# Two VectorE operations as one instruction, and the gate's products moved behind the sequence stage, in a gated FNet and Mish kernel

## The chip, the cores and the metric

The kernel runs on one core of a Trainium2 chip. The metric is the device time of one execution in microseconds. A program of this kind has five engines that work side by side, each through its own list of instructions in order: TensorE (PE in the profile; its weight loads are PEld), VectorE (DVE), ScalarE (ACT), GpSimd (POOL, here used to issue stores) and SyncE (SP, here used to issue loads). A matmul writes to one of eight banks of PSUM; VectorE and ScalarE read and write both PSUM and SBUF.

## The reference

With x of 2048 tokens by 640 features, four transform matrices, a dense layer of 1728 hidden units and a gate vector:

```
a   = einsum("bsd,ed->bse", x, dft_hid_re);  b = einsum("bsd,ed->bse", x, dft_hid_im)
y   = einsum("ts,bse->bte", dft_seq_re, a) - einsum("ts,bse->bte", dft_seq_im, b)
h   = einsum("bsd,df->bsf", x, w1) + b1
act = h * tanh(softplus(h))                      # Mish
g   = sigmoid((x * gate_w).sum(-1, keepdims=True))
out = g * y + (1 - g) * einsum("bsf,fd->bsd", act, w2)
```

All of it is float32.

## The kernel before

**Arithmetic.** Everything is held transposed, features on the partitions, in tiles of 128 x 512. A float32 operand is split into a high part (a copy to the format fp32r, made on ScalarE) and a low part (operand minus high part, a subtraction on VectorE); `operand` (L377) does this for a moving tile, `split` (L367) for weight blocks. A product of two blocks is three matmuls, high by high, high by low and low by high (`mm3`, L392). The block products themselves are saved by a scheme of sums and differences of blocks (seven products in place of eight), whose sums are again VectorE operations: `tt` (L350) records one `tensor_tensor` with three operands, and nearly all VectorE work goes through `tt`, `split` and `operand`.

**Stages.** The sequence stage multiplies x with the two sequence matrices and stores u; the hidden stage multiplies u with the hidden matrices, scales by g and stores y; the dense stage makes the rest of the first dense layer and Mish, and stores act; the last stage multiplies act with w2, adds y and writes the output. Parts of the first dense layer are made inside the sequence stage and stored in two halves, "early" and "late". `early_acts` (L1136) loads both halves for twelve tiles, adds them (one `tt` each, called the sums below), applies Mish on ScalarE and stores act. `make_x5` and `make_w5` prepare sums of x and w1 for products that are made at the start of the hidden stage (`five_units`).

**The gate.** `gates` (L1237) loads x once more, 16 tiles of 128 x 640, and makes for each one VectorE instruction (`scalar_tensor_tensor`, L1243) that multiplies by the gate vector and sums along the row. Then ScalarE loads the sigmoid's table, applies the sigmoid (L1248), VectorE makes 1 - g (L1249), SP writes both as rows to DRAM (grow and qrow, L1251), and ScalarE loads Mish's table again. The hidden stage reads grow back, spread over the partitions, when it scales its first results; qrow is read later.

**What sets the order.** Nothing is issued as the code is read. Every instruction is first recorded as an `Op` with its engine, its dependencies and a guess of its time, and `Graph.run` (L142) then plays the program through with these guesses and issues each instruction when it begins in that play. TensorE's order is fixed as recorded. For the other engines `wants` (L102) works out backwards, from the matmuls that need a result, when each operation should start (`want`); an operation whose inputs are there stands in its engine's list `ready`, sorted by `want`, and a free engine takes the first one that may have its buffers:

```
i = next((i for i, x in enumerate(line)
          if self.ops[x[1]].since <= now and granted(self.ops[x[1]], blocked)), None)
...
op.emit()
free[e] = now + op.hold
```

So operations are made ahead of their need, as far as buffers allow. Two settings put work that nobody waits for at a chosen time of the play: `since` (not before) and `by` (its due time). The constants `GATES = 60.0, 10.0` and `SUMS = 270.0, 12.0` are such times: start and step, for the 16 products and the 12 sums. The loads of the gate's tiles get `since` 20 us ahead of that. `AHEAD_OF` does the same for make_x5 and make_w5.

**Buffers.** `Pool`s hold tiles that are handed out in the play: ten pairs r (moving operands, high and low), 26 pairs w (weights), 18 tiles f and six wider tiles x in float32, and the eight banks. Each tile is a tile of its own for the framework that adds the waits between engines.

Of the kernel before, what the change touches and what calls it, by code (L numbers as in the profile page):

```python
# [28 lines left out]
DELAY = 3.3  # L29
RATE = 364e3  # L30
CALM, CALM_DMA, NEAR = 1.0, 3.0, 3.0
GATES = 60.0, 10.0
SUMS = 270.0, 12.0
SOON = 6.0
AHEAD_OF = 290.0, 30.0
WITHIN = 12.0
LEAD, LAG = 2, 2
# [19 lines left out]
class Op:  # L57


    def __init__(self, engine, emit, took, hold, at):  # L60
        self.engine, self.emit, self.took, self.hold, self.at = engine, emit, took, hold, at
        self.deps, self.after, self.vals = set(), [], []
        self.prompt, self.ends, self.want, self.psum, self.by, self.since = False, 0.0, None, False, 1e9, 0.0


class Graph:
# [35 lines left out]
    def wants(self):  # L102

        for op in self.ops:
            for d in op.deps:
                d.after.append(op)
            if op.engine == "PE":
                op.ends = op.at + op.took
                op.want = op.at
                continue  # L110
            op.prompt = op.psum or not op.fills and any(d.prompt and d.engine in ("ACT", "DVE") for d in op.deps)
            if op.prompt:
                op.ends = max([d.ends for d in op.deps if d.prompt or d.engine == "PE"], default=0) + op.took
                op.want = op.ends + (PROMPT if op.psum else LATER)
        back, todo, line = {}, {op.n: len(op.after) for op in self.ops}, []

        def reached(op):
            late = min(min([a.want for a in op.after], default=1e9) - HOP, op.by) - op.took
            if op.want is not None:
                late = op.at if op.engine == "PE" else min(op.want, late)  # L120
            heapq.heappush(line, (-late, -op.n))
        for op in self.ops:
            if not op.after:
                reached(op)
        while line:
            late, n = heapq.heappop(line)
            op, late = self.ops[-n], -late
            if op.engine == "PE":
                op.want = late
            else:  # L130
                e, held = ("DMA", op.moves) if op.engine in ("SP", "POOL") else (op.engine, op.hold)
                ends = min(late + op.took, back.get(e, 1e9))
                op.want, back[e] = ends - op.took, ends - held
            for d in op.deps:
                todo[d.n] -= 1
                if not todo[d.n]:
                    reached(d)
        for op in self.ops:
            if op.engine != "PE":
                op.want = max([op.want, op.since] + [(d.at if d.engine == "PE" else d.want) + d.took for d in op.deps])  # L140

    def run(self, pools):  # L142
# [44 lines left out]
        def take(v):  # L187
            p = v.pool
            if p.free:
                return p.free.pop(0)  # L190
            q = p.lender
            t = q.free.pop(0)
            v.home = q, t
            return q.part(t)

        def bequeath(p):
            if p.heir and not p.asks:
                p.heir.free += [p.part(t) for t in p.free]
                p.free = []

        tight = False
        while left:
            began = False
            for e, line in ready.items():
                if free[e] > now + 1e-9 or not line:
                    continue
                if e == "PE":
                    i = next((i for i, x in enumerate(line) if x[1] == pe[-1]), None)
                    if i is not None and not granted(self.ops[pe[-1]], set()):
                        i = None  # L210
                else:
                    blocked = set()
                    i = next((i for i, x in enumerate(line)
                              if self.ops[x[1]].since <= now and granted(self.ops[x[1]], blocked)), None)
                if i is None:
                    continue
                op = self.ops[line.pop(i)[1]]
                if e == "PE":
                    pe.pop()
                for v in op.vals:  # L220
                    if v.pool and v.t is None:
                        v.pool.asks.remove(v.ask)
                        if v.ask in v.pool.soon:
                            v.pool.soon.remove(v.ask)
                        v.t = take(v)
                        bequeath(v.pool)
                op.emit()
                free[e] = now + op.hold
                if e in ("SP", "POOL"):
                    dma = max(now + DELAY, dma) + op.moves  # L230
                    end = dma + 0.1
                else:
                    end = now + op.took + 0.03
                heapq.heappush(events, (end, op.n, False))
                left -= 1
                began = True
            if began:
                tight = False
# [38 lines left out]
def fnet_mish_gate(ctx: ExitStack, tc: tile.TileContext, xn, xt, c_re, c_im, wd_re, wd_im,  # L277
# [4 lines left out]
    dr = ctx.enter_context(tc.tile_pool(name="dr", bufs=1, space=bass.MemoryType.DRAM))  # L282
    ctx.enter_context(tc.manual_schedule())

    def pair(name, n):
        return sb.tile([P, n], F32R, name=f"{name}h"), sb.tile([P, n], F32R, name=f"{name}l")

    psum = Pool("psum", [pp.tile([P, N], F32, name=f"ps{i}") for i in range(8)])
    R = Pool("r", [pair(f"r{i}", N) for i in range(NR)])
    FS = Pool("f", [sb.tile([P, N], F32, name=f"f{i}") for i in range(NFS)])  # L290
    X = Pool("x", [sb.tile([P, D], F32, name=f"x{i}") for i in range(NX)], FS, lambda t: t[:, :N])
    FS.lender = X
    W = Pool("w", [pair(f"w{i}", D) for i in range(NW)], R, lambda t: (t[0][:, :N], t[1][:, :N]))
    b1s = Val(t=sb.tile([P, NF], F32, name="b1s"))
    gcol = Val(t=sb.tile([P, KS], F32, name="gcol"))
    qcol = Val(t=sb.tile([P, KS], F32, name="qcol"))
# [13 lines left out]
    def f32(t):  # L310
        return t.bitcast(F32)

    def whole(*vals):
        return [(v, None) for v in vals]

    def dve(emit, r, w, n=N, more=0.0):
        took = 0.15 + n / 960 + more
        return G.add("DVE", emit, r, w, took, took - 0.083)
# [26 lines left out]
    def add_to(d, t, v):  # L345

        o = place(d, t)
        dma("POOL", lambda: nc.gpsimd.dma_start(o.t, v.t, accum_op=OP.add), whole(v, o), whole(o), 2.8 * P * N * 4)

    def tt(o, a, b, op, cut=(slice(None),) * 3, rows=slice(None), n=N):  # L350
        (x, y, z) = cut
        dve(lambda: nc.vector.tensor_tensor(o.t[rows, x], a.t[rows, y], b.t[rows, z], op=op),  # L352
            whole(a, b), whole(o), n)

    def fresh(pool, a, b, op):
        o = Val(pool)
# [10 lines left out]
    def split(w, at, src, a=0, n=N):  # L367

        c = slice(at * P, at * P + n)
        s = slice(a, a + n)  # L370
        ks = range(at, at + n // P)
        hs, ls = [(w, (k, 0)) for k in ks], [(w, (k, 1)) for k in ks]
        act(lambda: nc.scalar.activation(w.t[0][:, c], src.t[:, s], AF.Copy), whole(src), hs, n)
        dve(lambda: nc.vector.tensor_tensor(w.t[1][:, c], src.t[:, s], f32(w.t[0][:, c]), op=OP.subtract),  # L374
            whole(src) + hs, ls, n)

    def operand(src, pool=None, alone=False):  # L377
        r = Val(pool or R)
        if alone:
            dve(lambda: nc.vector.tensor_copy(r.t[0][:, :N], src.t[:, :N]), whole(src), [(r, 0)], N // 2)  # L380
        else:
            act(lambda: nc.scalar.activation(r.t[0][:, :N], src.t[:, :N], AF.Copy), whole(src), [(r, 0)])  # L382
        dve(lambda: nc.vector.tensor_tensor(r.t[1][:, :N], src.t[:, :N], f32(r.t[0][:, :N]), op=OP.subtract),  # L383
            whole(src) + [(r, 0)], [(r, 1)])
        return r

    def mm(bank, w, k, wn, x, xn_, start, stop):
# [748 lines left out]
    def early_acts():  # L1136

        for i, key in enumerate(early):
            since = SUMS[0] + SUMS[1] * i
            o, v = (load_of(FS, d[key], since=since) for d in (early, late))  # L1140
            tt(o, o, v, OP.add)
            G.ops[-1].by = since + SUMS[1]
            out_act(key[1], key[0], o, o)
# [167 lines left out]
    early_rests()  # L1311
    for q in range(4):
        sq[q].second(seq.low)
        if q == 2:
            gates()
        sq[q].third()
        if q in UNITS:
            later = sq[q + 2]
            unit = Halves(seq, 0, 2, lambda t, k: c_tile(q)(t, k + KH), None, sq[q],
                          lambda d, t: load_of(FS, later.aside[min(d, 2)]), later.finish)  # L1320
            unit.done, unit.give = sq[q].done, sq[q].give
            for _ in unit.steps():
                pass
    jobs = [make_x5, lambda since: None, make_w5]
    for i, job in enumerate(jobs):
        job(AHEAD_OF[0] + AHEAD_OF[1] * i)
    early_acts()
    units = five_units()
    steps = (s for p in hd[::-1] for s in p.steps(hid.top))
    lines = [(s for u in line for s in u) for line in (units[::2], units[1:2])]  # L1330
# [74 lines left out]
```

## Time and profile before

| | |
|---|---|
| time, median of 3 runs | 849.57 us (849.28 to 850.17) |
| the profiled execution: time / span | 849.68 us / 847.6 us |
| granted TensorE clock, mean | 0.949 |
| instructions | 12444 |
| ScalarE busy | 533.8 us, 982 instructions |
| GpSimd busy | 122.0 us, 222 instructions |
| DMA | 239.42 MB, mean 282 GB/s |

The time of the profiled execution is longer than its span, which runs from the first to the last instruction of the trace. Busy time of VectorE counts a pipelined instruction from its start to its end, so back-to-back operations overlap a little. A row of a timeline gives start and duration in microseconds, then engine, line, operation, written and read tiles and a count. A row of the waits gives who waited, for whom, how long in all, how often, and the longest. A row of the groups gives the busy time, the mean duration in ns, and the idle time ahead of the group.

### The profile page before, as it was taken

Reading aid. Unit: us, or ns where it says so; the run is one execution under the profiler, and the core shown is the slowest. Engines: PE = TensorE matmul, PEld = TensorE weight load, DVE = VectorE, ACT = ScalarE, POOL = GpSimd, SP = SyncE. Lnnn points to the kernel's source line nnn. Section 1 sums busy time; section 2 is a strip of 40 time slices with the busy share of each in tenths; the row PEclk is TensorE's granted clock in tenths of the full one; section 3 lists DMA queues with packets and bytes.
Section 4 is the critical chain, followed back from the end, with each engine's and each line's share of the span. In section 5 each row is a group of like instructions: output and inputs, shape, how many; then the busy total and the mean of one; then the engine's idle time right before and its main releaser. Section 6 shows DMA issues by size and latency. Waiting matters only on the chain.

```text
span 847.6 us, 12444 instructions
## 1 busy us (share of the span) xinstructions
PE 842.1 (99%) x3703; PEld 694.1 (82%) x3703; DVE 746.3 (88%) x1357; ACT 533.8 (63%) x982; POOL 122.0 (14%) x222
## 2 busy tenths in 40 slices
PE   9999999999999999999999999999999999999998
PEld 7888888888888888888888888888878888888886
DVE  7978889999988899999897999997586999899984
ACT  6966765767563854665588754755577877646432
POOL 0122110010100121130012102012333121011200
PEclk9999999999999999999999999999999999999999
DMA  9899686968764999999788876768789798969963
GB/s 332 323 342 329 200 281 197 386 230 293 262 186 137 321 312 362 341 372 379 263 282 311 337 246 230 245 210 295 245 296 405 266 347 280 306 181 297 318 212 139
DMA packets 119123, 239.42 MB, mean 282 GB/s; under 512 B 15232, under 2 KB 23168, under 8 KB 119056
## 3 DMA queue, kind: packets, MB, share of 16 engines
q1 hardware_dynamic: 101072, 182.32, 63.1%
q0 software_dynamic: 17840, 56.18, 18.8%
q8 instruction: 29, 0.48, 0.2%
q14 instruction: 38, 0.31, 0.1%
q10 hardware_dynamic: 144, 0.13, 0.0%
HBM read 179.77 MB, written 58.80 MB: 281 GB/s over the span
## 4 chain that ended last, share of the span: by engine, by line
PE 97%; DVE 2%; DMA 0%; issue 0%; ACT 0%; SPq 0%; DVEq 0%
PE ps L388 97%; DVE f L352 1%; DMA f<-in_c_im_dram 0%; DVE w10l L383 0%; DVE r4l L383 0%; DVE r3l L383 0%; DVE r1l L383 0%; DVE r2l L383 0%; ACT f L361 0%; DVE w13l L374 0%; DVE w12l L383 0%; ACT ps L361 0%; DVE r0h L380 0%; DVE x L705 0%; ACT x L703 0%
## 5 line engine op out<-in xcount | busy, mean ns | idle before, releaser
L352 DVE TENSOR_TENSOR f<-f,f 128x512 f32<-128x512 f32 (+2 forms) x314 | 202.7, 660 | 4.5 <-ACT f L847 3.3
L361 ACT ACTIVATE f<-ps 128x512 f32<-128x512 f32 x143 | 83.7, 596 | 40.6 <-PE ps L388 27.8
L352 DVE TENSOR_TENSOR f<-ps,f 128x512 f32<-128x512 f32 x96 | 64.1, 687 | 23.1 <-PE ps L388 20.2
L343 POOL DMA_DIRECT2D act<-f x52 | 28.3, 544 | 133.4 <-ACT f L847 110.6
L361 ACT ACTIVATE ps<-f 128x512 f32<-128x512 f32 x70 | 40.8, 595 | 8.6 <-DVE f L352 8.3
L382 ACT ACTIVATE r9h<-f 128x512 fp32r<-128x512 f32 x40 | 25.2, 631 | 28.4 <-DVE f L352 15.2
L847 ACT ACTIVATE f<-f,b1s 128x512 f32<-128x512 f32 x36 | 26.0, 722 | 21.4 <-DVE f L352 21.1
L382 ACT ACTIVATE r5h<-f 128x512 fp32r<-128x512 f32 x41 | 25.9, 631 | 21.3 <-PE ps L388 10.0
L382 ACT ACTIVATE r8h<-f 128x512 fp32r<-128x512 f32 x42 | 26.5, 631 | 16.8 <-PE ps L388 7.1
L382 ACT ACTIVATE r6h<-f 128x512 fp32r<-128x512 f32 x39 | 24.6, 631 | 18.5 <-PE ps L388 11.3
L382 ACT ACTIVATE r1h<-f 128x512 fp32r<-128x512 f32 x37 | 23.3, 629 | 20.3 <-DVE f L352 9.1
L352 DVE TENSOR_TENSOR x<-x,x 128x256 f32<-128x256 f32 (+3 forms) x80 | 34.2, 448 | 2.1 <-DMA x<-in_xn_dram 1.1
L382 ACT ACTIVATE r2h<-f 128x512 fp32r<-128x512 f32 x40 | 25.2, 631 | 16.0 <-DVE f L352 8.8
L382 ACT ACTIVATE r7h<-f 128x512 fp32r<-128x512 f32 x39 | 24.5, 627 | 15.6 <-PE ps L388 10.6
L383 DVE TENSOR_TENSOR r5l<-f,r5h 128x512 fp32r<-128x512 f32 x41 | 28.1, 687 | 5.9 <-ACT r5h L382 5.8
L382 ACT ACTIVATE r3h<-f 128x512 fp32r<-128x512 f32 x36 | 22.7, 630 | 16.1 <-PE ps L388 11.0
L343 POOL DMA_DIRECT2D u<-f x28 | 15.2, 544 | 122.1 <-DVE f L352 49.9
L382 ACT ACTIVATE r4h<-f 128x512 fp32r<-128x512 f32 x40 | 25.2, 629 | 11.8 <-PE ps L388 7.4
L382 ACT ACTIVATE r0h<-f 128x512 fp32r<-128x512 f32 x37 | 23.3, 629 | 13.9 <-DVE f L352 7.6
L383 DVE TENSOR_TENSOR r7l<-f,r7h 128x512 fp32r<-128x512 f32 x39 | 26.8, 687 | 5.9 <-ACT r7h L382 5.8
L383 DVE TENSOR_TENSOR r2l<-f,r2h 128x512 fp32r<-128x512 f32 x40 | 27.5, 687 | 4.1 <-ACT r2h L382 4.0
L383 DVE TENSOR_TENSOR r8l<-f,r8h 128x512 fp32r<-128x512 f32 x42 | 28.8, 686 | 1.2 <-ACT r8h L382 1.2
(2463 smaller groups left out, 2824.4 us busy)
## 6 DMA issues: line engine op xcount, KB each, us to landing
f<-in_c_im_dram SPq DMA_DIRECT2D x102, 256.0 KB, 4.8
f<-in_c_re_dram SPq DMA_DIRECT2D x102, 256.0 KB, 5.1
f<-act SPq DMA_DIRECT2D x72, 256.0 KB, 5.3
f<-u SPq DMA_DIRECT2D x60, 256.0 KB, 5.1
act<-f POOLq DMA_DIRECT2D x52, 256.0 KB, 4.5
f<-in_xt_dram SPq DMA_DIRECT2D x40, 256.0 KB, 4.2
x<-in_xn_dram SPq DMA_DIRECT2D x24, 320.0 KB, 5.0
u<-f POOLq DMA_DIRECT2D x28, 256.0 KB, 5.5
```

Source lines behind the costliest of these rows:

```text
L343: dma(queue, lambda: ISSUE[queue].dma_start(d.t, v.t[:rows]), whole(v), whole(d), rows * N * 4)
L352: dve(lambda: nc.vector.tensor_tensor(o.t[rows, x], a.t[rows, y], b.t[rows, z], op=op), whole(a, b), whole(o), n)
L361: act(lambda: nc.scalar.activation(o.t, a.t, AF.Copy, scale=scale), whole(a), whole(o))
L382: act(lambda: nc.scalar.activation(r.t[0][:, :N], src.t[:, :N], AF.Copy), whole(src), [(r, 0)])
L383: dve(lambda: nc.vector.tensor_tensor(r.t[1][:, :N], src.t[:, :N], f32(r.t[0][:, :N]), op=OP.subtract), whole(src) + [(r, 0)], [(r, 1)])
L388: G.add("PE", lambda: nc.tensor.matmul(bank.t, w.t[wn][:, k * P:k * P + P], x.t[xn_][:, :N], start, stop, skip_group_check=True), [(w, (k, ...
L847: act(lambda: nc.scalar.activation(o.t[rows], src.t[rows], AF.Mish, **more), whole(src, table) + whole(b1s) * bias, whole(o), more=0.1)
```

## The change

Three things are done.

First, all tiles f and x become slices of one large tile `flat`, all r and w slices of one large tile `cut`, and the eight banks slices of one PSUM tile `banks`. So the distance between any two tiles of a kind is a number of elements, and one access pattern can cover two of them.

Second, an operation `tensor_tensor` gets a `form`: the arithmetic, the number of elements, and which operands lie in which memory. When VectorE takes an operation in the play, the planner looks through the list of ready ones for another of the same form whose tiles are near enough and whose buffers are free. If there is one, both are issued as one instruction over two pieces (`two`). The planner counts the second's time less `PAIR`, 0.067 us. If the first is wanted within 1 us (`EASE`), only a mate wanted within 1 us of it (`CLOSE`) is taken. `HELD` multiplies by 1.0 and so does nothing.

Third, `gates()` is recorded behind `early_acts()` and not inside the sequence stage, its products are due from 380 us on in steps of 4 (before: from 60 in steps of 10), and the sums from 200 on in steps of 10 (before: from 270 in steps of 12).

```diff
-GATES = 60.0, 10.0
-SUMS = 270.0, 12.0
+GATES = 380.0, 4.0
+SUMS = 200.0, 10.0
 SOON = 6.0
+PAIR = 0.067
+EASE, CLOSE = 1.0, 1.0
+REACH = 1 << 15
+HELD = {"DVE": 1.0}
...
+                begin(op)
+                if op.form:
+                    blocked = set()
+                    for i, (want, n) in enumerate(line):
+                        o = self.ops[n]
+                        if op.want - now < EASE and want - op.want > CLOSE:
+                            break
+                        if (o.form == op.form and o.since <= now and abs(o.spot() - op.spot()) < REACH
+                                and granted(o, blocked)):
+                            line.pop(i)
+                            begin(o)
+                            op.mate = o
+                            break
                 op.emit()
-                free[e] = now + op.hold
+                more = op.mate.hold - PAIR if op.mate else 0.0
+                free[e] = now + op.hold + more
...
-                    end = now + op.took + 0.03
+                    end = now + op.took + more + 0.03
...
+    flat = sb.tile([P, NFS * N + NX * D], F32, name="flat")
+    cut = sb.tile([P, 2 * (NR * N + NW * D)], F32R, name="cut")
+
+    def pieces(mem, n, m, at=0):
+        return [mem[:, at + i * n:at + i * n + n] for i in range(m)]
...
+    psum = Pool("psum", pieces(pp.tile([P, 8 * N], F32, name="banks"), N, 8))
+    R = Pool("r", pairs(N, NR))
+    FS = Pool("f", pieces(flat, N, NFS))
...
+    def two(a, b):
+
+        return bass.AP(a.tensor, a.offset, [a.ap[0], [b.offset - a.offset, 2], a.ap[1]])
+
+    def elementwise(aps, alu, r, w, n):
+
+        def emit():
+            o, a, b = aps()
+            if op.mate:
+                o, a, b = (two(*p) for p in zip((o, a, b), op.mate.aps()))
+            nc.vector.tensor_tensor(o, a, b, op=alu)
+        op = dve(emit, r, w, n)
+        op.aps = aps
+        kinds = [v.pool.name if v.pool else "" for v, _ in w[:1] + r[:2]]
+        if all(kinds):
+            o = w[0][0]
+            op.form = alu, n, kinds[0] in "rw", *("psum" == k for k in kinds)
+            op.spot = lambda: o.t[1].offset if op.form[2] else 0
+        return op
...
-        if q == 2:
-            gates()
         sq[q].third()
...
     early_acts()
+    gates()
     units = five_units()
```

`tt`, `split` and `operand` record their `tensor_tensor` through `elementwise`; `tt` takes the form away where it covers fewer than 128 partitions.

More of the change, by code (lines that the diff above doesn't have):

```diff
@@ L63, in __init__ @@
         self.prompt, self.ends, self.want, self.psum, self.by, self.since = False, 0.0, None, False, 1e9, 0.0
+        self.form, self.mate = None, None
 class Graph:
@@ L132, in wants @@
                 ends = min(late + op.took, back.get(e, 1e9))
-                op.want, back[e] = ends - op.took, ends - held
+                op.want, back[e] = ends - op.took, ends - held * HELD.get(e, 1.0)
             for d in op.deps:
@@ L194, in take, with begin @@
             return q.part(t)
+        def begin(op):
+            for v in op.vals:
+                if v.pool and v.t is None:
+                    v.pool.asks.remove(v.ask)
+                    if v.ask in v.pool.soon:
+                        v.pool.soon.remove(v.ask)
+                    v.t = take(v)
+                    bequeath(v.pool)
         def bequeath(p):
@@ L219, in run @@
                     pe.pop()
[L220 to L226, printed above, removed]
+                begin(op)
[11 more added lines that the diff above has]
+                            break
                 op.emit()
-                free[e] = now + op.hold
+                more = op.mate.hold - PAIR if op.mate else 0.0
+                free[e] = now + op.hold + more
                 if e in ("SP", "POOL"):
@@ L232, in run @@
                 else:
-                    end = now + op.took + 0.03
-                heapq.heappush(events, (end, op.n, False))
-                left -= 1
+                    end = now + op.took + more + 0.03
+                for o in (op, op.mate) if op.mate else (op,):
+                    heapq.heappush(events, (end, o.n, False))
+                    left -= 1
                 began = True
@@ L283, in fnet_mish_gate, with pairs @@
     ctx.enter_context(tc.manual_schedule())
[L285 to L291, printed above, removed]
+    flat = sb.tile([P, NFS * N + NX * D], F32, name="flat")
+    cut = sb.tile([P, 2 * (NR * N + NW * D)], F32R, name="cut")
+    def pieces(mem, n, m, at=0):
+        return [mem[:, at + i * n:at + i * n + n] for i in range(m)]
+    def pairs(n, m, at=0):
+        t = pieces(cut, n, 2 * m, at)
+        return list(zip(t[::2], t[1::2]))
+    psum = Pool("psum", pieces(pp.tile([P, 8 * N], F32, name="banks"), N, 8))
+    R = Pool("r", pairs(N, NR))
+    FS = Pool("f", pieces(flat, N, NFS))
+    X = Pool("x", pieces(flat, D, NX, NFS * N), FS, lambda t: t[:, :N])
     FS.lender = X
-    W = Pool("w", [pair(f"w{i}", D) for i in range(NW)], R, lambda t: (t[0][:, :N], t[1][:, :N]))
+    W = Pool("w", pairs(D, NW, 2 * NR * N), R, lambda t: (t[0][:, :N], t[1][:, :N]))
     b1s = Val(t=sb.tile([P, NF], F32, name="b1s"))
@@ L348, in add_to @@
         dma("POOL", lambda: nc.gpsimd.dma_start(o.t, v.t, accum_op=OP.add), whole(v, o), whole(o), 2.8 * P * N * 4)
+    def two(a, b):
[14 more added lines that the diff above has]
+        return op
     def tt(o, a, b, op, cut=(slice(None),) * 3, rows=slice(None), n=N):
         (x, y, z) = cut
-        dve(lambda: nc.vector.tensor_tensor(o.t[rows, x], a.t[rows, y], b.t[rows, z], op=op),
-            whole(a, b), whole(o), n)
+        made = elementwise(lambda: (o.t[rows, x], a.t[rows, y], b.t[rows, z]), op, whole(a, b), whole(o), n)
+        if rows != slice(None):
+            made.form = None
     def fresh(pool, a, b, op):
@@ L373, in split @@
         act(lambda: nc.scalar.activation(w.t[0][:, c], src.t[:, s], AF.Copy), whole(src), hs, n)
-        dve(lambda: nc.vector.tensor_tensor(w.t[1][:, c], src.t[:, s], f32(w.t[0][:, c]), op=OP.subtract),
-            whole(src) + hs, ls, n)
+        elementwise(lambda: (w.t[1][:, c], src.t[:, s], f32(w.t[0][:, c])), OP.subtract, whole(src) + hs, ls, n)
     def operand(src, pool=None, alone=False):
@@ L382, in operand @@
             act(lambda: nc.scalar.activation(r.t[0][:, :N], src.t[:, :N], AF.Copy), whole(src), [(r, 0)])
-        dve(lambda: nc.vector.tensor_tensor(r.t[1][:, :N], src.t[:, :N], f32(r.t[0][:, :N]), op=OP.subtract),
-            whole(src) + [(r, 0)], [(r, 1)])
+        elementwise(lambda: (r.t[1][:, :N], src.t[:, :N], f32(r.t[0][:, :N])), OP.subtract,
+                    whole(src) + [(r, 0)], [(r, 1)], N)
         return r
```

## The prediction

> **What bounds the kernel now.** First the profile's page.
>
> ```profile
> span 847.6 us, 12444 instructions
> ...
> PE 842.1 (99%) x3703; PEld 694.1 (82%) x3703; DVE 746.3 (88%) x1357; ACT 533.8 (63%) x982; POOL 122.0 (14%) x222
> ...
> PEclk9999999999999999999999999999999999999999
> ```
>
> TensorE looks full, VectorE (DVE) nearly so. But a matmul's row is longer than the distance to the next one, so 99% could hide gaps. The timeline of TensorE decides: below are the first and the last row of a stretch that shows 197 matmuls (196 distances), and then the last matmul of the program. The chain of waits gives the first real one.
>
> ```profile
> 499.73 0.39 PE L388 MATMUL ps<-r1h,w1l 128*128 128x512 f32 x1
> ...
> 544.16 0.39 PE L388 MATMUL ps<-r8h,w22h 128*128 128x512 f32 x1
> ```
>
> ```profile
> 843.12 0.39 PE L388 MATMUL ps<-r5h,w25l 128*128 128x512 f32 x1
> ```
>
> ```profile
> 4.42 615.62 PE ps L388 x2712
> ...
> 635.56 207.96 PE ps L388 x916
> ```
>
> A clean distance is (544.16 - 499.73) / 196 = 0.22668 us. Of the 3703 matmuls 8 are the warm-up, so 3695 run from 4.42 to 843.12: 3694 distances need 837.36 us, and 838.70 passed. **All stalls of TensorE between its first and its last real matmul are 1.34 us.** Ahead of them lie 4.42 us (first load, first copy), behind them 847.6 - 843.1 = 4.5 us (last matmul, last copies, last store). The profiled execution took 849.68 us, 2.1 more than its span; the median of the three runs, 849.57, is 0.11 lower.
>
> Which stalls these are, by the waits of TensorE (behind the warm-up) and of its weight loads, and the largest of them in the timelines of TensorE and ScalarE and in the chain:
>
> ```profile
> PE ps L388 <- ACT ps L361: 0.3, 1, 0.3
> PE ps L388 <- DVE r0h L380: 0.3, 1, 0.3
> ```
>
> ```profile
> PEld ps L388 <- ACT ps L361: 0.7, 1, 0.7
> PEld ps L388 <- DVE ps L352: 0.4, 1, 0.4
> PEld ps L388 <- DVE f L352: 0.3, 1, 0.3
> PEld ps L388 <- DVE x L352: 0.2, 1, 0.2
> ```
>
> ```profile
> 634.85 0.39 PE L388 MATMUL ps<-r4h,w5l 128*128 128x512 f32 x1
> 635.56 0.50 PE L388 MATMUL ps<-r3h,w23h 128*128 128x512 f32 x1 [0.33 <-ACT ps L361]
> 635.90 0.39 PE L388 MATMUL ps<-r3l,w23h 128*128 128x512 f32 x1
> ```
>
> ```profile
> 633.90 0.63 ACT L382 ACTIVATE r9h<-f 128x512 fp32r<-128x512 f32 x1
> ...
> 634.92 0.59 ACT L361 ACTIVATE ps<-f 128x512 f32<-128x512 f32 x1
> ```
>
> ```profile
> 620.74 0.68 DVE w10l L383
> ...
> 633.26 0.61 DVE f L352
> ```
>
> At 634.85 the next two distances are 0.71 and 0.34 in place of 0.227: 0.59 us, nearly half of all stalls, because the bank's start value (the copy at 634.92) came late, behind the copy of r9h; and the chain that led to that copy ran on VectorE from 620.74 to 633.87, with short breaks alone. Elsewhere TensorE waits three times on a VectorE result, each wait partly hidden. So VectorE is busy but not late: its work is made ahead. This bounds every gain: with all stalls gone the profiled time is 849.68 - 1.34 = 848.34, the median 848.2. A measurement of this kernel can tell about 0.2% from no change, 1.70 us: faster means below 847.87, slower above 851.27. The stalls do not hold that much.
>
> **The change part by part.** *Pairs.* What one instruction over two tiles saves is VectorE's fixed cost, read from the starts of back-to-back operations:
>
> ```profile
> 193.42 0.69 DVE L352 TENSOR_TENSOR f<-f,f 128x512 f32<-128x512 f32 x1
> 194.02 0.42 DVE L374 TENSOR_TENSOR w2l<-f,w2h 128x256 fp32r<-128x256 f32 x1
> 194.36 0.42 DVE L374 TENSOR_TENSOR w6l<-f,w6h 128x256 fp32r<-128x256 f32 x1
> ```
>
> 512 elements hold the engine for 0.60 us, 256 for 0.34, so an element costs about 0.26/256 = 1.0 ns and an instruction about 0.08 us beside. The diff's planner takes 0.067, near enough. How many pairs the planner finds no row tells: the ends are none, and half of nearly all 1357 operations, some 625. I take 300, in the middle: the plan draws operations early, so several of a kind usually stand ready. That is 300 x 0.07 = 21 us of VectorE's 746, with ends 0 and 44. On the end of the kernel it takes nothing directly: the 746 lie beside TensorE's unbroken row. What it can remove is stall, at most the 1.34; on the other side the first tile of a pair comes late by the second tile's 512 elements, 0.53 us. Everything behind a pair on VectorE's queue also waits for the later of the two sets of inputs: ScalarE's high parts or TensorE's banks. The planner pairs only what it holds ready, so where the chip keeps the plan this wait is nought.
>
> The rows where this can hurt are those that read a bank:
>
> ```profile
> L352 DVE TENSOR_TENSOR f<-ps,f 128x512 f32<-128x512 f32 x96 | 64.1, 687 | 23.1 <-PE ps L388 20.2 <-ACT f L361 1.7 <-ACT w10h L382 0.8
> L352 DVE TENSOR_TENSOR ps<-ps,f 128x512 f32<-128x512 f32 x25 | 17.0, 695 | 7.8 <-ACT x L361 7.2 <-ACT f L361 0.6
> ```
>
> TensorE's next group into a bank waits for such a row to end. Three waits of this sort exist (0.4, 0.3, 0.2 above), so at three places the lead is already nil. At each, a pair whose first tile is the wanted one adds up to 0.53 us; a pair that brings the wanted tile forward takes away up to as much. Between -0.9 and +1.6 I take +0.1: the planner puts an urgent operation only with one wanted within 1 us. The Trainium skill (PSUM — Partial Sum Buffer, PSUM bank collisions raise a hardware error) has a rule that speaks against such pairs: two engines must be kept apart by whole bank, so an instruction over two banks shuts TensorE out of both until it ends. The three waits agree; by that rule alone, with every one of the three lengthened, the sum would be the +1.6.
>
> *One large tile in place of many.* The bytes that a matmul reads are as many as before and its distance does not depend on names; I put this at nought. The trace does not show whether waits are kept by piece or by whole tile, since before no instruction spans two; that is a rival below.
>
> *The gate's products moved.* Sixteen operations on 640 elements and their loads:
>
> ```profile
> 197.44 0.82 DVE L1243 SCALAR_TENSOR_TENSOR x<-x,x 128x640 f32<-128x640 f32 x1
> 198.18 0.08 DVE L1243 DVE_READ_ACCUMULATOR x<-x,x 128x1 f32 x1
> 198.18 0.69 DVE L383 TENSOR_TENSOR r1l<-f,r1h 128x512 fp32r<-128x512 f32 x1
> ```
>
> ```profile
> 197.93 1.28 ACT L1247 ACT_TABLE_LOAD   x1
> ```
>
> ```profile
> L333 SPq DMA_DIRECT2D f<-grow x4: 319/374/600, 480.4 to 549.8; - x4
> L1251 SPq DMA_DIRECT2D grow<-gcol x1: 390/390/390, 200.5 to 200.5; - x1
> ```
>
> Each holds VectorE for 0.74 us, 11.8 in all, now due from 60 to 210 us of the plan, then from 380 to 440. The gate's row of numbers, written at 200.5, is first read at 480.4. In the new place the last product is due at 440 and the row is out a few us later: some 35 us to spare, so the later gate itself delays nobody. With the products move a sigmoid, two table loads on ScalarE of 1.28 us (the first is shown) and two small stores on SP; ScalarE is busy for 41.6 of the 64 us from 380 to 444 (row below), so they fit. The twelve sums with their Mish go from 270-414 to 200-320, also away from their readers. The crossing on the queues: 16 loads of 320 KB (5.2 MB over 60 us, 87 GB/s) join SP's queue around 360-420, while three of the twelve sums leave the part behind 378 (24 loads and 12 stores of 256 KB over 144 us, 66 GB/s while they last); POOL's queue only gains room there. Here are the stretches concerned (VectorE busy, granted clock, DMA share, GB/s), then one with all engines, VectorE third:
>
> ```profile
> 180.00:200.00 20.00, 20.00 (x44) 0.95 0.83 292
> 200.00:220.00 20.00, 20.00 (x36) 0.95 0.87 281
> ```
>
> ```profile
> 380.00:400.00 20.00, 18.11 (x32) 0.95 1.05 394
> ...
> 420.00:440.00 20.00, 19.24 (x43) 0.95 0.85 287
> 440.00:460.00 20.00, 14.02 (x30) 0.95 0.94 343
> ```
>
> ```profile
> 380.00:444.00 64.00, 64.00 (x284) 52.97 (x284) 57.59 (x112) 41.61 (x84) 5.97 (x11) 0.95 0.88 308
> ```
>
> From 380 to 444 VectorE has 64.0 - 57.6 = 6.4 us free. In come 11.8, out go three sums of 0.60, and if pairs are as frequent as I took them, 25 of them save 1.7: 11.8 - 1.8 - 1.7 = 8.3, so 1.9 us too much, without pairs 3.6. It must be made before 380 or after 444, where the row of 440-460 has 6.0 us free. The cover is that operands are made ahead; that a VectorE without a free moment need not stall TensorE is shown by 180-220: both rows are full, and the chain runs on TensorE alone through them. The ends for this part are 0 and the whole 3.6; I take 0.1. Loads that slip are covered by the 35 us for the gate, and the transfers sum to at most 394 + 87 - 66 = 415 GB/s for a moment.
>
> *The stall at 634.85.* The copy of r9h waits for the VectorE rows of the chain from 620.74 on; a pair brings it forward by 0.07, and eight would do. I take 0.5 of its 0.59 as gone, and say what is late next: the three waits on VectorE rows.
>
> *Sum.* 849.68 - 0.5 + 0.1 (banks) + 0.1 (crowding) = 849.3 for the profiled execution, 849.2 for the median.
>
> **The rivals.**
>
> *A. The gate crowds the start of the hidden stage: slower.* For it speaks the sum above, 1.9 to 3.6 us over, and that the plan is thinnest there. VectorE ends the low part of w14 at 443.92, and TensorE reads it at 443.97:
>
> ```profile
> 443.50 0.42 DVE L374 TENSOR_TENSOR w14l<-x,w14h 128x256 fp32r<-128x256 f32 x1
> ```
>
> ```profile
> 443.97 0.39 PE L388 MATMUL ps<-r8h,w14l 128*128 128x512 f32 x1
> ```
>
> Against it: the planner weighs both in one queue and can draw the products forward. It decides once what is pushed back exceeds the lead of the operand pushed, here 0.05 us. Price: 1.9 to 3.6 less the 0.5 of the other stall: 851.0 to 852.7.
>
> *B. Pairs hold TensorE's tiles back: slower.* Wherever the wanted tile is first and has less than 0.53 us of lead. Three places are known; six would cost 3.2: 850.7 to 852.3. Against it: only three waits in 3695 matmuls.
>
> *C. Waits by whole tile.* If a pair of banks orders itself against what lies between them, some 60 pairs of the 121 rows with a bank would each stop TensorE by up to 0.53: 32 us, 881. Against it: the two pieces are given with their step, not as one range.
>
> *D. Few pairs form*, or none on the path: 849.6.
>
> *E. VectorE is the true bound.* Then its 21 us come off: 829. For it speaks only that its 88% exceeds the weight loads' 82%; against it the 196 distances without a gap. The Trainium skill (Perfetto Trace Analysis, Identifying the Most-Contended Engine) would have TensorE judged by its weight loads and not by matmul busy time, which is how this case arises; the trace disagrees, as the distances show no room at the granted clock of 0.95.
>
> **How the numbers follow.** Forecast 0.70, A 0.15 (0.10 of it above 851.27), B 0.05 (taken whole as slower), C 0.02, D 0.05, E 0.03. Faster is E alone, 0.03; slower is 0.10 + 0.05 + 0.02 = 0.17; the rest, 0.80, cannot be told from no change. The time is the forecast's, 849.2. The range goes from 848.2, all stalls gone, to 852.0, which takes in most of A and B; C and E stay out.
>
> **What would show it.** Right: the same 3703 matmuls at 0.2267; VectorE busy near 725 with about 1050 instructions and rows of about 1.2 us; the gap at 634.85 gone; no wait of TensorE above 0.5 us; products between 380 and 440. Wrong: a wait of TensorE on a VectorE row between 400 and 460 (A), many short ones on rows that read banks (B, C), a stretch of changed distance or clock, or a head or tail that differs from 4.4 and 4.5 us.

## The result and the profile after

The changed kernel takes 852.95 us (median of 6 runs, 852.59 to 853.67), the kernel before 849.87 in the same job (849.28 to 850.42): a ratio of 1.0037 with a 95% interval of 1.0024 to 1.005. It is slower by 3.1 us, outside the range that was given, and on the side that had a chance of 0.17.

The profiled execution took 852.59 us. In the rows of the changed kernel all tiles f and x are called flat, all r and w cut, all banks banks; its matmuls are at L437 and its `tensor_tensor` at L389, and each edit below shifts these lines a little. The page:

```profile
span 850.8 us, 12304 instructions
...
PE 843.1 (99%) x3703; PEld 694.2 (82%) x3703; DVE 737.2 (87%) x1202; ACT 532.8 (63%) x982; POOL 122.0 (14%) x222
...
PEclk9999999999999999999999999999999999999999
```

The matmuls are as many as before. VectorE lost 155 instructions and 9 us, so the pairs are there and do what they should on their own engine. The span still grew by 3.2 us. The groups of VectorE by shape show where the pairs are; 512-element pairs are those written as 128x1024:

```profile
L389 DVE TENSOR_TENSOR cut<-flat,cut 128x1024 fp32r<-128x1024 f32 x46 | 55.8, 1220 | 0.2 <-ACT cut L431 0.2
L389 DVE TENSOR_TENSOR flat<-flat 128x1024 f32<-128x1024 f32 x32 | 39.0, 1219 | 0.0
...
L389 DVE TENSOR_TENSOR flat<-banks,flat 128x1024 f32<-128x1024 f32 x10 | 12.2, 1220 | 0.7 <-PE banks L437 0.4
```

A pair takes 1.22 us where two rows of 0.69 stood 0.60 apart. Only ten of them read PSUM. Now TensorE's waits and those of its weight loads:

```profile
PE banks L437 <- DVE flat L389: 2.9, 4, 1.3
```

```profile
PEld banks L437 <- DVE flat L389: 4.8, 5, 1.7
```

Before, no wait of TensorE behind the warm-up was above 0.3 us; now one line of VectorE holds it four times. The chain of waits, which before ran on TensorE from 4.42 to 620, tells where. It is cut to the pieces that matter:

```profile
45.83 168.76 PE banks L437 x743
214.59 0.03 issue
214.62 0.02 DVEq L389
214.64 0.04 issue
214.69 1.24 DVE flat L389
215.92 0.04 issue
215.97 358.89 PE banks L437 x1582
574.86 0.02 issue
574.88 1.24 DVE flat L389
576.12 0.04 issue
576.16 209.38 PE banks L437 x921
785.55 0.02 issue
785.57 1.24 DVE flat L389
786.81 0.04 issue
786.85 59.92 PE banks L437 x263
```

The same thing happens three times. TensorE finishes a matmul, a VectorE instruction of 1.24 us starts within 0.1 us of that, and TensorE goes on 0.04 us after it ends. All three are pairs that read banks. The timelines of TensorE and VectorE around the second:

```profile
573.32 1.52 PE L437 MATMUL banks<-cut 128*128 128x512 f32 x6
576.16 0.50 PE L437 MATMUL banks<-cut 128*128 128x512 f32 x1 [1.32 <-DVE flat L389]
```

```profile
572.39 2.09 DVE L389 TENSOR_TENSOR cut<-flat,cut 128x512 fp32r<-128x512 f32 x2
574.88 1.23 DVE L389 TENSOR_TENSOR flat<-banks,flat 128x1024 f32<-128x1024 f32 x1 [0.41 <-PE banks L437]
```

Both engines stand still in turn: VectorE for 0.41 us until TensorE's matmul is done, then TensorE for 1.32. From the starts of single matmuls, less the usual distance of 0.227, TensorE loses 0.87, 1.48 and 0.80 us at the three places and 0.11 at each restart, 3.48 us in all. A fourth wait, at 45.24, costs 0.47. Against that the stall that lay at 634.85 (0.59) is nearly gone.

**What the built programs say.** Of the ten pairs that read PSUM, seven read one bank twice. The other three read two banks: 1 and 6, 1 and 5, 3 and 5. In the program's list of instructions the first waits for a matmul into bank 4, which neither of its halves touches, and the next matmul into bank 4 waits for the pair; the second pair is tied in the same way to a matmul into bank 3, and the third holds back a matmul into bank 4. Each of these banks lies between the two that are read. So the waits that the framework adds are kept for the range from the first bank to the last. This is rival C of the prediction (the expectations below call the rivals theories A, B and C). Nothing in the planner keeps the two banks near: `REACH` limits only the distance of written tiles r and w.

The same lists explain the three sizes. At the second place the next matmul of TensorE is already one into bank 3, which has to wait: from the start of the last matmul, at 574.46, to the next, at 576.16, 1.70 us pass, which hold that matmul (to 574.86), the pair and two short hand-overs. At the first and the third place TensorE still has three matmuls into a bank outside the range (bank 0 and bank 2) and makes them while the pair runs: 3 x 0.227 = 0.68 us, the difference between 1.48 and 0.80.

### The profile page after: what moved, and what is told of

It reads as the page before. It is cut to its first block, busy times and chain, and to the rows that moved or that the text cites. A ratio compares the mean times of both kernels' runs of the same rounds, so it can differ in the third digit from the quotient of the medians.

```text
span 850.8 us, 12304 instructions
## 1 busy us (share of the span) xinstructions
PE 843.1 (99%) x3703; PEld 694.2 (82%) x3703; DVE 737.2 (87%) x1202; ACT 532.8 (63%) x982; POOL 122.0 (14%) x222
## 4 chain that ended last, share of the span: by engine, by line
PE 94%; DMA 3%; DVE 2%; issue 0%; ACT 0%; SPq 0%; DVEq 0%
PE banks L437 94%; DMA flat<-in_xt_dram 1%; DMA flat<-in_c_re_dram 1%; DVE flat L389 1%; DVE cut L389 1%; DMA flat<-in_c_im_dram 1%; DMA b1s<-in_b1b_dram 0%; SPq L362 0%; ACT cut L431 0%; DVE flat L754 0%; ACT flat L752 0%; DVEq L389 0%
## 5 line engine op out<-in xcount | busy, mean ns | idle before, releaser
L437 PE MATMUL banks<-cut 128*128 128x512 f32 x3695 | 839.5, 389 | 2.9 <-DVE flat L389 2.9
L437 PEld LDWEIGHTS banks<-cut 128*128 128x128 f32 x3695 | 693.2, 188 | 149.7 <-DVE flat L389 4.8
L389 DVE TENSOR_TENSOR cut<-flat,cut 128x512 fp32r<-128x512 f32 (+4 forms) x581 | 390.1, 702 | 49.0 <-ACT cut L431 41.2
L431 ACT ACTIVATE cut<-flat 128x512 fp32r<-128x512 f32 x475 | 290.4, 628 | 208.4 <-PE banks L437 96.4
L389 DVE TENSOR_TENSOR flat<-flat 128x512 f32<-128x512 f32 (+4 forms) x433 | 278.9, 666 | 6.8 <-ACT flat L896 2.9
L411 ACT ACTIVATE flat<-banks 128x512 f32<-128x512 f32 x168 | 97.8, 596 | 47.8 <-PE banks L437 37.1
L389 DVE TENSOR_TENSOR flat<-banks,flat 128x512 f32<-128x512 f32 (+1 forms) x101 | 73.1, 739 | 23.7 <-PE banks L437 19.7
L423 ACT ACTIVATE cut<-flat 128x256 fp32r<-128x256 f32 (+4 forms) x182 | 81.1, 480 | 7.7 <-DVE flat L389 6.6
L372 POOL DMA_DIRECT2D act<-flat x52 | 28.3, 544 | 154.7 <-ACT flat L896 128.5
L411 ACT ACTIVATE banks<-flat 128x512 f32<-128x512 f32 x75 | 43.6, 594 | 9.9 <-DVE flat L389 9.0
L389 DVE TENSOR_TENSOR banks<-banks,flat 128x512 f32<-128x512 f32 x35 | 23.5, 696 | 16.5 <-ACT flat L411 16.2
```

Of the source, the lines that this page charges most:

```text
L372: dma(queue, lambda: ISSUE[queue].dma_start(d.t, v.t[:rows]), whole(v), whole(d), rows * N * 4)
L389: nc.vector.tensor_tensor(o, a, b, op=alu)
L411: act(lambda: nc.scalar.activation(o.t, a.t, AF.Copy, scale=scale), whole(a), whole(o))
L437: G.add("PE", lambda: nc.tensor.matmul(bank.t, w.t[wn][:, k * P:k * P + P], x.t[xn_][:, :N], start, stop, skip_group_check=True), [(w, (k, ...
```

## The experiments

**The same plan with the banks numbered anew.** The planner's order, its pairs and its tiles stay as they are. Only where the eight banks lie in PSUM changes, so that the pairs of two banks read neighbours:

```diff
-    psum = Pool("psum", pieces(pp.tile([P, 8 * N], F32, name="banks"), N, 8))
+    banks = pieces(pp.tile([P, 8 * N], F32, name="banks"), N, 8)
+    psum = Pool("psum", [banks[i] for i in (4, 1, 5, 3, 6, 2, 0, 7)])
```

> The changed kernel with the same order of all instructions and the same pairs; only the eight banks are numbered anew, so that each of the three pairs that read two different banks reads two neighbours (0 and 1, 1 and 2, 2 and 3) and no bank lies between. Theory C (a pair is ordered against all banks between its two): the waits of TensorE of 0.87, 1.48 and 0.80 us at these pairs go with their restarts of 0.11 each, 3.5 us in all: 849.3 to 849.7 us. Theory B (a pair holds its own tiles too long, whatever lies between): nothing changes, 852.6 to 853.3. Theory A (the gate crowds its new place): nothing changes.

Measured: 849.50 us against 849.79 before, ratio 0.9998 (0.9989 to 1.0007). The loss is gone. The timelines of TensorE and VectorE at the second place:

```profile
572.72 4.47 PE L438 MATMUL banks<-cut 128*128 128x512 f32 x19
```

```profile
572.38 1.49 DVE L390 TENSOR_TENSOR cut<-flat,cut 128x1280 fp32r<-128x1280 f32 x1
573.78 1.81 DVE L390 TENSOR_TENSOR flat<-banks,flat 128x1024 f32<-128x1024 f32 x2
```

The same pair starts right behind the instruction ahead of it, waits for nothing, and 19 matmuls pass without a break. It is as long as before and holds its two banks as long, so theory B falls: what cost time was the order against the banks between, not the length. At the other two places TensorE does not stop either. The chain runs on TensorE from the last early wait to the end:

```profile
46.27 797.31 PE banks L438 x3515
```

**The same plan with the banks far apart,** in the order (2, 0, 3, 1, 4, 6, 7, 5), pairs of 0 and 7, 0 and 6, 1 and 6:

> As before it, but the banks are numbered so that the three pairs lie as far apart as they can (0 and 7, 0 and 6, 1 and 6). Theory C: more banks lie between, so each of the three still stops TensorE, for as long or longer, since the pair now waits for later matmuls and ScalarE copies too: 853 to 855. Theory B and theory A: nothing changes, 852.6 to 853.3.

Measured: 854.47 us against 849.79, ratio 1.0055 (1.0042 to 1.0068). The three stops stay and grow to 1.55, 1.53 and 1.53 us plus the restarts, 4.9 us; the kernel is 5.0 us slower than with neighbouring banks. In the built program TensorE now has no matmul outside the range in hand at any of the three, so each costs about what only the second cost before. TensorE's waits:

```profile
PE banks L438 <- DVE flat L390: 4.1, 3, 1.4
```

**Only one pair far apart,** order (2, 1, 3, 7, 4, 6, 0, 5):

> The changed kernel with the same order and pairs, banks numbered so that two of the three pairs read neighbours and the pair at the end of the hidden stage (574.88 in the changed kernel's trace) reads banks 1 and 6, with four between. Theory C: one stop of TensorE at that pair, 0.9 to 1.7 us, and none at the other two places: 850.4 to 851.2. Theory B: 849.5 as with neighbours, or 853 as in the changed kernel, since the pairs are the same.

Measured: 850.29 us against 849.79, ratio 1.0006 (0.9997 to 1.0015), 0.8 more than with all three near, a little below what was expected. By the time alone this can't be told from the kernel before; the trace is clear. Of three places one stops, the one chosen:

```profile
572.71 2.20 PE L438 MATMUL banks<-cut 128*128 128x512 f32 x9
575.60 1.66 PE L438 MATMUL banks<-cut 128*128 128x512 f32 x6 [0.69 <-DVE flat L390]
```

The last of the nine matmuls starts at 574.52, so TensorE loses 0.85 and 0.11, here again with three matmuls into a bank outside the range. The cost is paid per place.

**The same plan with three pairs, or all pairs, issued as two instructions.** In `emit`, the mate is issued behind the first where it is so decided:

```diff
-            if op.mate:
-                o, a, b = (two(*p) for p in zip((o, a, b), op.mate.aps()))
+            late = None
+            if op.mate:
+                both = list(zip((o, a, b), op.mate.aps()))
+                if any(q and x.offset != y.offset for (x, y), q in zip(both, op.form[3:])):
+                    late = op.mate
+                else:
+                    o, a, b = (two(*p) for p in both)
             nc.vector.tensor_tensor(o, a, b, op=alu)
+            if late:
+                late.emit()
```

Three pairs split:

> The changed kernel with the same order and the same banks; the three pairs that read two different banks are issued as two instructions, one behind the other, and the other 152 pairs stay. Theory C: as with neighbouring banks, 849.3 to 849.7. Theory B: those three and none of the 152 were harmful, also 849.3 to 849.7, and better than with neighbouring banks by up to 1.6 us if the length of the pair matters by itself. Theory A: 852.6 to 853.3.

All pairs split:

> The changed kernel with the same order; each of the 155 pairs is issued as two instructions, so VectorE has some 10 us more to do than the plan counts with. Theory C: no wait on banks between, 849.3 to 850.5, the upper end if the plan needs the saved time somewhere. Theory A: 852.6 to 853.3 or more, since VectorE is fuller. If the saved VectorE time is what the end needs: above 853.

Measured: 849.46 us with three split (ratio 0.9996, 0.9987 to 1.0005) and 850.40 with all split (1.0006, 0.9997 to 1.0015), both against 849.79. So the three pairs carry the whole loss, and the other 152, of which 145 touch SBUF alone, none that is seen. With three split the chain runs on TensorE through all three places:

```profile
4.53 838.83 PE banks L444 x3695
```

Three split is as good as neighbouring banks, to 0.04 us by the medians: the length of the pair costs nothing that is seen here. All split costs 0.9 us more, and TensorE's waits show it: with three split there is one of 0.2 us, with all split VectorE's line holds it twice for 0.8, early in the program:

```profile
42.16 4.37 PE L437 MATMUL banks<-cut 128*128 128x512 f32 x18 [0.51 <-DVE flat L387]
46.77 1.43 PE L437 MATMUL banks<-cut 128*128 128x512 f32 x5 [0.24 <-DVE flat L387]
```

This fits a plan that counts with the saved time and needs it where it has no lead; which split pairs are late there was not tried.

**The parts of the change one by one.** Large tiles alone, with the old plan (all of the edit below); the move alone (its first lines); pairs alone, with the old times (the rest):

```diff
-                if op.form:
+                if op.form and False:
...
-GATES = 380.0, 4.0
-SUMS = 200.0, 10.0
+GATES = 60.0, 10.0
+SUMS = 270.0, 12.0
...
+        if q == 2:
+            gates()
...
     early_acts()
-    gates()
```

Large tiles alone:

> The kernel before, with its order, its gate and its sums where they were, and no pairs; only the tiles are slices of three large ones. If slices of a large tile cost nothing while no instruction covers two of them (prediction, and theory C): no change, 849.3 to 849.9. If waits were kept for the large tile as a whole: far slower, above 880.

The move alone:

> Large tiles and the gate and the sums at their new times, no pairs. Theory A (the gate crowds its new place, and pairs are needed to make room): a wait of TensorE between 380 and 460, 850.5 to 853. Theory C: the move costs nothing that is seen, 849 to 850.

Pairs alone:

> Large tiles and pairs, the gate and the sums at their old times; the plan that comes out has one pair that reads two banks far apart (1 and 7), at the end of the hidden stage's second problem half. Theory C: one stop of TensorE of 0.9 to 1.6 us there and no other: 850.3 to 851.2. Theory A: as before, 849.5. Theory B: no rule for the number, but the other pairs of the stage hold back too.

Measured, against 849.67: large tiles 849.59 (0.9998, 0.9989 to 1.0006), the move 850.38 (1.0009, 1.0 to 1.0018), pairs 853.01 (1.0037, 1.0024 to 1.0049).

Slices of large tiles cost nothing while no instruction covers two of them, as expected. The move without pairs costs 0.7 us, at the edge of what the interval tells; this lies between what theories A and C had said. The loss is not where theory A had it: the two main stops lie ahead of all that was moved in:

```profile
31.95 1.43 PE L437 MATMUL banks<-cut 128*128 128x512 f32 x5 [0.67 <-ACT flat L411]
```

```profile
46.96 1.43 PE L437 MATMUL banks<-cut 128*128 128x512 f32 x5 [0.43 <-DVE flat L389]
```

Pairs alone missed the number. The stop that was expected at 575 is there (1.12 us and the restart). A second one, not expected, is at 192, 1.61 us and the restart, where no pair of two banks stands:

```profile
193.81 0.50 PE L437 MATMUL banks<-cut 128*128 128x512 f32 x1 [1.45 <-ACT banks L411]
```

The run with the old times below was made for it.

**Pairs within one bank only,** in the planner, with the new times and with the old:

```diff
                         if (o.form == op.form and o.since <= now and abs(o.spot() - op.spot()) < REACH
+                                and (not any(op.form[3:]) or op.bank() == o.bank())
...
+            op.bank = lambda: [v.t.offset for v in (w[0][0], r[0][0], r[1][0]) if v.pool.name == "psum"]
```

With the new times:

> The changed kernel, where the planner pairs two reads of PSUM only if both read the same bank, so it plans the three pairs as single instructions. Theory C: 849.2 to 849.6, as with neighbouring banks. What is left to gain is the rest of TensorE's stalls, about 1 us.

With the old times:

> Pairs, of PSUM reads only within one bank, and the gate and the sums at their old times. Theory C says that of the two stops of the run with pairs alone the one at 575 goes (1.2 us). The one at 192 had no pair of two banks near it: if it comes from the plan and its stores it stays, 851.5 to 852; if it had to do with the two banks it goes too, 849.3 to 849.7.

Measured: 849.31 us against 849.67 with the new times (0.9996, 0.9988 to 1.0005), 851.40 against 849.79 with the old (1.0021, 1.0012 to 1.003). With the old times the stop at 575 is gone:

```profile
572.83 4.47 PE L439 MATMUL banks<-cut 128*128 128x512 f32 x19
```

The one at 192 stays, though in the profiled execution, the fastest of the eleven, only with 0.64 us and the restart. Timelines of TensorE and ScalarE there:

```profile
192.56 1.65 PE L439 MATMUL banks<-cut 128*128 128x512 f32 x6 [0.48 <-ACT banks L413]
```

```profile
190.39 0.60 ACT L413 ACTIVATE flat<-banks 128x512 f32<-128x512 f32 x1 [1.06 <-DMA u<-flat]
...
191.92 0.59 ACT L413 ACTIVATE banks<-flat 128x512 f32<-128x512 f32 x1
```

ScalarE's copy waits for the store of u out of the tile that it writes, and the start value of TensorE's bank comes behind it. The eleven times of this kernel lie 3.4 us apart (850.47 to 853.87). No pair of two banks is left in it, so this stop has nothing to do with two banks; that it comes from the stores is read from these rows, and why they are late was not tried. The version with pairs within one bank and the new times has the lowest time: 3.4 us below the changed kernel by the differences to their own runs of before (-0.36 against +3.08). It is not to be told from neighbouring banks (-0.29), three pairs split (-0.33) or the kernel before.

## Why the prediction was wrong

**The step that failed** is "One large tile in place of many ... I put this at nought", and in rival C the sentence "the two pieces are given with their step, not as one range". The waits are kept by range from bank to bank, as the lists of the built program say and the runs with the banks renumbered show. That term is 3.4 us (after: +3.08 to its runs of before, neighbouring banks: -0.29) and not 0. It alone made the kernel slower. Whether the chip needs the waits on the banks between was not tried: no run reads two banks apart without them. C was named, but with the price of 60 pairs, 32 us, and a chance of 0.02. Both sizes were off: three pairs read two banks in place of 60, since only ten pairs formed that read PSUM and seven of these read one bank, and each cost about 1.1 us, twice the 0.53 per place. The 0.53 counted the second tile's length alone; what is lost is the way there and back: a matmul into one of the banks of the range ends, the whole pair runs, TensorE starts again, less the matmuls into other banks that it can make meanwhile.

**What bounds the kernel** was right and made the reading easy: the same 3703 matmuls, no room for a gain. All stops taken together are 1.34 us before. After, the first matmul starts at 4.42 and the last 0.39 ahead of the chain's 786.85 + 59.92, which is 841.96, and 3694 distances of 0.22668 leave 4.6 us of stops. They grew by 3.3, the span by 3.2.

**Pairs.** What a pair saves was right, 0.07 us. The number was not: 155 in place of 300, and VectorE at 737 us in place of 725. It cost the forecast nothing, since that time lay beside TensorE.

**Rival B** was worked out for pairs that hold their own tiles. The runs with neighbouring banks and with three pairs split agree to 0.04 us, and in neither does TensorE stop at the three places, so this was nil, and the +0.1 for banks too.

**Rival A** was argued from a sum that came out 1.9 us over with pairs. It did not happen. TensorE has no wait from 380 to 460, and VectorE (third figure of the row) was not full:

```profile
400.00:420.00 20.00, 20.00 (x90) 16.57 (x89) 17.92 (x32) 8.95 (x16) 1.08 (x2) 1.00 0.91 318
420.00:440.00 20.00, 20.00 (x90) 16.58 (x89) 18.38 (x35) 17.11 (x34) 1.62 (x3) 1.00 0.97 323
```

The sum took the due times as the times of work. The planner drew the products forward, as it may, and the gate's row was out early:

```profile
L1292 DVE SCALAR_TENSOR_TENSOR flat<-flat x16: 816/820/826, 366.6 to 425.7; 128x640 f32<-128x640 f32 x16
```

```profile
L1300 SPq DMA_DIRECT2D grow<-gcol x1: 376/376/376, 428.5 to 428.5; - x1
```

**The stall at 634.85** went, as said: 0.09 us of its 0.59 is left, at 637.76. The prediction put this down to pairs alone, and the runs say otherwise. By the starts of the matmuls the stall is 0.62 us with large tiles alone, 0.26 with the move alone, 0.42 with pairs within one bank at the old times, and 0.09 with both. So the number was in part luck. What came next was not the three known waits but a new one at 45.24 (0.47), long before the gate or the sums; a new plan moves the small stops about by some tenths. What a new plan costs by itself, 0.7 us with the move alone and 1.6 with pairs within one bank at the old times, had no term in the sum; only the range left room for it.

**Rival E** has no support left: with neighbouring banks VectorE's 9 us are off, the three stops too, and the time is that of before.

## What to carry to other kernels

Before one instruction is laid over two tiles, look at what lies between them: if waits are kept by range, as for the banks here, it is ordered against everything there, and on the engine that sets the end this costs the full way there and back. The built program's list of waits shows it before anything is run. Renumbering the buffers, with the plan untouched, tests it cleanly and may be the whole cure. In a kernel whose bound engine has almost no gaps, an easier life for another engine can gain almost nothing; judge such a change first by the new waits it can bring, and expect that every new plan shifts the small ones.

## What the runs showed of the hardware

The recorded clock of TensorE was 0.949 in the profile of before and 1.000 in that of after, and the distance between matmuls was the same: 358.89 us for 1582 of them after, 0.227 each, as before. The kernel before too was later seen at 0.999 to 1.000, with spans of 847.0 to 849.5, against 847.6 at 0.949. So the sentence of the prediction that there was no room "at the granted clock of 0.95" read too much into that row; what sets the 0.2267 us was not tried.

An instruction over two tiles of 512 took 1.22 us whether it read SBUF alone or PSUM too: the means of the 46, 32 and 10 of them agree within 1 ns. Behind each of the three stops of the changed kernel the first matmul is followed by the next after 0.33 to 0.34 us in place of 0.227: a restart costs 0.11.
